# A fused attention, gated block and Fourier layer: the last 64 rows of a product by high and low parts side by side, and one tile of a norm loaded earlier

## The chip, the cores and the metric

The kernel runs on one core of one Trainium2 chip, in one launch. The metric is device microseconds of an execution; the median of three runs is given, and one more execution was recorded by the hardware profiler.

## The reference, cut to what matters

Three layers follow one another, all in fp32: attention in a window of 64, a gated block whose gate mixes over the sequence, and a Fourier layer with a norm and a feed-forward part. Batch is 4, the sequence S = 576, the model width 512.

```python
def _attn_ref(q, k, v):                     # (4, 8, 576, 64)
    ...                                     # softmax over rel in [0, 64)

def _moe_ref(x, w_in, w_spatial, b_spatial, w_out):
    h = np.maximum(x @ w_in, 0.0)           # w_in: 512 x 1024
    u, v = (h[..., :d_ff // 2], h[..., d_ff // 2:])
    v_n = (v - mean(v)) / np.sqrt(var(v) + 1e-06)
    v_s = np.einsum('ts,bsd->btd', w_spatial, v_n) + b_spatial[None, :, None]
    return (u * v_s) @ w_out

def _moe2_ref(x, w_ch1, w_ch2):             # w_ch1: 512 x 2048
    X = np.fft.fft(np.fft.fft(x, axis=1), axis=2)
    u = x + np.real(X)
    un = (u - mean(u)) / np.sqrt(var(u) + 1e-06)
    return u + np.maximum(un @ w_ch1, 0.0) @ w_ch2
```

## The kernel before, in words

**Precision.** Products are made of parts: a value is split into a rounded high part and the low rest, and a product of two values is three matmuls, high by high, high by low and low by high (`PASS`). `hi_lo` makes the parts: ACT copies the value into the high one, and one or two ticks later POOL (in places DVE) subtracts it from the value for the low one.

**One batch of the gated block.** x lies transposed in `xg`, 512 features on 4 x 128 partitions, with both parts. `b_v(b, m)` makes the value half for 128 rows (m = 0 to 3) or the last 64 (m = 4): 4 blocks of features by 3 passes, twelve matmuls of 512 columns into `ps_v` (L509). ACT takes the Relu into a `tr` buffer `vr` (L513), DVE the statistics of the norm (L487, L488), POOL the reciprocal root (L493, L494), DVE applies it in place (L498), and the parts go to the region `vn` of the resident array `ar`, those of the last 64 rows to its end, `vt` (L524 to L527). `b_u` makes the gate (`ps_u`, L539; ACT L542). `part_c` mixes over the sequence (`ps_c`, L552), then DVE multiplies by the gate into a `tr` buffer `gf` (L557), ACT copies its high part (L209) and POOL subtracts for the low one (L213). `part_d` is w_out (`ps_d`, L567). The Fourier steps follow.

**Buffers.** The pool `tr` has five buffers of 128 x 512 and one name for all of its users: `vr`, `gf`, the decoded weights `dec`, the norm's tiles `uu` and others. Weights come as 64-bit numbers: SP loads them (L222) into `raw_tile(0)`, `raw_tile(1)` or a staging buffer (all called `st`), ACT and DVE turn them into fp32 in a `dec` buffer (L230 to L243), and ACT and POOL make the parts (L209, L211). A raw tile holds two norm tiles of 128 x 512, its halves.

**The norm chains.** A tile of the Fourier layer's norm has four steps: `s0` loads 128 rows of `u_scr` (L754 on SP), `s1` takes the statistics on DVE and the root on POOL, `s2` applies them (DVE L498), `s3` transposes the tile on PE into `ps_un` (L783), and ACT and DVE make its parts (L787, L789). Chain 0 has three tiles, whose `s0` takes a `tr` buffer; chain 1 has three, in the halves of `raw_tile(1)` in turn.

**The order.** The engines' instructions stand in the order in which the program is written out. For each batch it follows a string, `ORDER_0` to `ORDER_3`: `i` is the next piece of the batch's block, `u` one of the gate, `s` a step of the next batch's attention, `n` one step of the weights' decoding, `a` a tick for what was put off, `c` and `d` the next step of chain 0 and of chain 1. Batch 3 has no attention beside it; there the weights of the feed-forward part are decoded and the chains' first tiles worked. The order of chain 0's steps comes from `staggered` (L884), that of chain 1 is a list (L898).

Of the kernel before, what the change touches and what calls it, by code (L numbers as in the profile page):

```python
# [9 lines left out]
F32 = mybir.dt.float32  # L10
# [3 lines left out]
AF = mybir.ActivationFunctionType  # L14
ALU = mybir.AluOpType
# [26 lines left out]
           "aannnnnnnaaaannannaaaiannaainninanniianaaaaaaaaaannsannnannnnnnnnnnananainnvnaasannnqv")  # L42
ORDER_1 = ("iiisuuuusiisuauquvqusiisiaiiiivsiiqvssaviiiasqaiasviaiiaiiiqsiiiiaiiiiiqsv")
ORDER_2 = ("iiisuuuusiisuauquvqusiisiaiiiivsiiqvssaviiiasaiasviaiqiaiiiqsiiiiaiiiiiqsv")
ORDER_3 = ("iniccnnncOiannuucnannnauucnnnnnnnnniciuucnnnunnaaaaaunanniddicaciciaaicaaaaaininindcindiniddaindinda"
           "idaindinidiiiiaidiaiiaiii")
ORDER = (ORDER_0, ORDER_1, ORDER_2, ORDER_3)

# [67 lines left out]
def tile_kernel(ctx: ExitStack, tc: tile.TileContext, q, k, v, w_in, w_sp, b_sp, w_out, w_c1, w_c2,  # L116
                rows, ident, mask, t1h, t1l, s2c, s2s, out):
    nc = tc.nc
    act, dve, pool, pe, sp = nc.scalar, nc.vector, nc.gpsimd, nc.tensor, nc.sync
# [5 lines left out]
    def raw_tile(i):  # L125
        return st_p.tile([128, 512], I64, tag=f"st{i}", name="st")
# [19 lines left out]
    def psO(nm="psO"):  # L146
        return ps_o.tile([128, 512], F32, tag="o", name=nm)

    def tr(nm, shape=(128, 512), dt=F32):
        return tr_p.tile(list(shape), dt, tag="tr", name=nm)  # L150
# [13 lines left out]
                 vn=5400, x0=4 * 2 * S, x1=4608)  # L164
    off, n = {}, 0
# [5 lines left out]
    def region(nm, o, n):  # L171
        return ar[:, off[nm] + o:off[nm] + o + n]

    wi = region("wi", 0, sizes["wi"]).rearrange("p (f k a c) -> p f k a c", f=8, k=4, a=2)
# [14 lines left out]
    PASS = ((0, 0), (0, 1), (1, 0))  # L189
# [4 lines left out]
    def later(n, fn):  # L194
        due.append((tick[0] + n, fn))
# [9 lines left out]
    def hi_lo(x, hi, lo, first=0, second=1, lo_eng=None):  # L205
        if first:
            later(first, lambda: act.activation(out=hi, in_=x, func=AF.Copy))
        else:
            act.activation(out=hi, in_=x, func=AF.Copy)  # L209
        if second == 0:  # L210
            (lo_eng or pool).tensor_tensor(out=lo, in0=x, in1=hi.bitcast(F32), op=ALU.subtract)  # L211
            return
        later(second, lambda: (lo_eng or pool).tensor_tensor(out=lo, in0=x, in1=hi.bitcast(F32), op=ALU.subtract))  # L213
# [270 lines left out]
    def norm_stats(x, n):  # L484
        st = sm_p.tile([128, 6], F32, tag="bn", name="bn")
        mv = sm_p.tile([128, 2], F32, tag="mv", name="mv")
        dve.bn_stats(out=st[0:n], in_=x[0:n])  # L487
        dve.bn_aggr(out=mv[0:n], in_=st[0:n])  # L488
        return mv

    def norm_rstd(mv, n):
        rs = sm_p.tile([128, 2], F32, tag="rs", name="rs")
        pool.tensor_scalar(out=rs[0:n, 0:1], in0=mv[0:n, 1:2], scalar1=1.0, scalar2=EPS, op0=ALU.mult, op1=ALU.add)  # L493
        pool.tensor_tensor(out=rs[0:n, 1:2], in0=rs[0:n, 0:1], in1=phalf[0:n], op=ALU.pow)  # L494
        return rs

    def norm_apply(x, mv, rs, n):
        dve.tensor_scalar(out=x[0:n], in0=x[0:n], scalar1=mv[0:n, 0:1], scalar2=rs[0:n, 1:2],  # L498
                          op0=ALU.subtract, op1=ALU.mult)

    def b_v(b, m):
        xt = xg[b % 2]
        n = 128 if m < 4 else 64
        ps = psO("ps_v")
        pf = ps.rearrange("p (f c) -> p f c", f=4)
        c = 0
        for kt in range(4):
            for a, w in PASS:
                pe.matmul(pf[0:n], lhsT=xt[:, kt, a, m * 128:m * 128 + n], rhs=wi[:, 4:8, kt, w],  # L509
                          start=(c == 0), stop=(c == 11))  # L510
                c += 1
        vr = tr("vr")
        act.activation(out=vr[0:n], in_=ps[0:n], func=AF.Relu)  # L513
        mv = norm_stats(vr, n)

        box = []
        later(1, lambda: box.append(norm_rstd(mv, n)))

        def finish():
            norm_apply(vr, mv, box[0], n)  # L520
            if m < 4:
                hi_lo(vr, vn[:, m, 0], vn[:, m, 1], 0, 1)
            else:
                act.activation(out=vt[0:64, 0], in_=vr[0:64], func=AF.Copy)  # L524
                act.activation(out=vt[0:64, 1], in_=vr[0:64], func=AF.Copy)
                pool.memset(vt[64:128, 1].bitcast(F32), 1.0)
                later(1, lambda: pool.tensor_tensor(out=vt[64:128, 0], in0=vr[0:64],  # L527
                                                    in1=vt[0:64, 0].bitcast(F32), op=ALU.subtract))

        later(2, finish)  # L530
# [183 lines left out]
    ff_slot, a2, un2, early_u, st2_ctx = {}, [], [], [], ExitStack()  # L714
# [4 lines left out]
    def un_parts(c):  # L719

        if c == 0:
            return [(0, 4, ar, at_x)]
        if c == 1:
            return [(0, 4, ar, at_y)]
        if c == 3:
            return [(0, 3, ar, at_x), (3, 4, ar, at_y + 1024)]
        return [(0, 2, un2[0], 0), (2, 3, ar, at_x + 3072), (3, 4, ar, at_y + 3072)]

    def un_of(c, part):
        m0, m1, x, o = part  # L730
        n = TILES[c] * 128
        return x[:, o:o + 2 * n * (m1 - m0)].rearrange("p (m a t) -> p m a t", a=2, t=n)
# [18 lines left out]
    def load_u(c, i, u=None):  # L751
        u = tr("uu") if u is None else u
        r0 = (FIRST[c] + i) * 128
        sp.dma_start(out=u, in_=u_scr[r0:r0 + 128, :])  # L754
        return u

    def norm_chain(c, i):
        box = {}

        def s0():  # L760
            if c == 1:
                if i == 0:
                    early_u.append(raw_tile(1).bitcast(F32))
                box["u"] = load_u(c, i, early_u[0][:, 512 * (i % 2):512 * (i % 2) + 512])
            else:
                box["u"] = load_u(c, i)

        def s1():
            box["mv"] = norm_stats(box["u"], 128)
            box["rs"] = norm_rstd(box["mv"], 128)  # L770

        def s2():
            norm_apply(box["u"], box["mv"], box["rs"], 128)

        def s3():
            u = box["u"]
            if c == 2 and not un2:
                st2_ctx.close()
                un2_p = ctx.enter_context(tc.tile_pool(name="un2", bufs=1))
                un2.append(un2_p.tile([128, 2048], F32R, name="un2"))  # L780
            ps = (psS if c == 2 else psT)("ps_un").rearrange("p (m c) -> p m c", m=4)
            for m in range(4):
                pe.transpose(ps[:, m, :], u[:, m * 128:(m + 1) * 128], idt)  # L783
            cc = slice(i * 128, i * 128 + 128)
            parts = [(un_of(c, p), ps[:, p[0]:p[1]]) for p in un_parts(c)]
            for un, x in parts:
                act.activation(out=un[:, :, 0, cc], in_=x, func=AF.Copy)  # L787
            for un, x in parts:
                dve.tensor_tensor(out=un[:, :, 1, cc], in0=x, in1=un[:, :, 0, cc].bitcast(F32), op=ALU.subtract)  # L789

        return [s0, s1, s2, s3]

    def ch1(c, j, h):
# [65 lines left out]
    with tc.manual_schedule():  # L859
# [19 lines left out]

        chain0, chain1 = ([norm_chain(c, i) for i in range(TILES[c])] for c in range(2))  # L880
        tables = (t1[:, 0], t1h), (t1[:, 1], t1l), (tc2, s2c), (ts2, s2s)
        chain_at = (0, 3, 4, 8)

        def staggered(chain):  # L884
            return [f[j] for n in range(40) for i, f in enumerate(chain) for j in range(4) if chain_at[j] + 6 * i == n]

        def start_w_out():
            st_next[:] = [lambda: raw_tile(0), lambda: raw_tile(1)]
            queue_units([w_out_unit(kt) for kt in range(4)])
            sp.dma_start(out=rix, in_=rows)  # L890
# [4 lines left out]
               "P": iter([lambda t=t: prep_w_sp(t) for t in range(5)]),  # L895
               "T": iter([lambda o=o, i=i: pool.dma_start(out=o, in_=i) for o, i in tables]),
               "b": iter([load_bias]), "B": iter([prep_bias]), "W": iter([start_w_out]),
               "O": iter([open_a2]), "c": iter(staggered(chain0)), "d": iter([chain1[i][j] for i, j in ((0, 0), (1, 0), (0, 1), (0, 2), (0, 3), (1, 1), (2, 0),  # L898
                                                            (1, 2), (1, 3), (2, 1), (2, 2), (2, 3))])}
        simple = {"s": attn_step, "n": nudge, "a": advance}  # L900
        for b in range(B):
# [12 lines left out]
        for g, group in enumerate(GROUPS):  # L914
# [7 lines left out]
            chain = [norm_chain(c, i) for c in nxt for i in range(TILES[c])]  # L922
            per = 2 if g == 0 else 3
            at = (0, 2, 3, 4) if g == 0 else (0, 1, 2, 3)
            start = N - 1 - at[3] - per * (len(chain) - 1)
            ul = {}
            for n in range(N + 1):
                if n < N:
                    c, j = steps[n]
# [51 lines left out]
```

## Time and profile before

| | |
|---|---|
| median of 3 runs | 815.94 us (815.81 to 817.22) |
| the profiled execution | 818.4 us, span 816.6 us |
| mean granted TensorE clock | 0.978 |
| PE busy | 783.4 us, 96% of the span |
| DVE, ACT, POOL busy | 414.8, 292.1, 238.8 us |

The rows below come from the profiled execution; their times count from the span's start. A row's bracket says how long the engine had stood idle before it and what ended that.

### The profile page before, as it was taken

What the parts mean: (1) busy time and instruction counts of PE and PEld (TensorE: products, weight loads), DVE (VectorE), ACT (ScalarE), POOL (GpSimd) and SP (SyncE); (2) the same over time, 40 slices, a digit from 0 to 9 for tenths busy, and PEclk for the clock granted to TensorE, in tenths of its full rate; (3) what the DMA queues carried; (4) which work ended last, traced back from release to release, by engine and by line L of the source; (5) the groups of instructions that cost most, each with busy time, mean ns of one, the idle gap of its engine ahead of it and who ended that gap; (6) DMA issues with size and microseconds to landing.
All of it is one profiled execution on the core that took longest, in us unless ns stands there. A gap on an engine that the chain in (4) does not pass through costs nothing.

```text
span 816.6 us, 13834 instructions
## 1 busy us (share of the span) xinstructions
PE 783.4 (96%) x5257; PEld 681.1 (83%) x5257; DVE 414.8 (51%) x1058; ACT 292.1 (36%) x867; POOL 238.8 (29%) x315
## 2 busy tenths in 40 slices
PE   6788999999999999997999999999999999999998
PEld 4557898889998999897889999888888888888886
DVE  3886765744473446565769888941212222221112
ACT  5556655545554544333433333320111111111100
POOL 1656462445424541444233333412000100010000
PEclk9679999999999999998999999999999999999999
DMA  8736426321223110422133445232000300020001
GB/s 207 178 71 173 125 62 166 92 49 43 58 71 73 31 27 26 137 91 65 50 134 116 125 126 154 77 117 78 14 14 13 116 14 13 14 78 26 0 1 51
DMA packets 89557, 62.79 MB, mean 77 GB/s; under 512 B 64978, under 2 KB 77522, under 8 KB 89492
## 3 DMA queue, kind: packets, MB, share of 16 engines
q1 hardware_dynamic: 87796, 55.29, 24.4%
q0 software_dynamic: 1696, 6.63, 2.4%
q8 instruction: 41, 0.67, 0.3%
q14 instruction: 24, 0.20, 0.1%
HBM read 52.47 MB, written 9.44 MB: 76 GB/s over the span
## 4 chain that ended last, share of the span: by engine, by line
PE 83%; DVE 7%; DMA 3%; ACT 3%; POOL 2%; issue 1%; SPq 1%; POOLq 0%; ACTq 0%; DVEq 0%
PE ps_y L824 24%; PE ps_h L800 24%; PE ps_v L509 6%; PE ps_d L567 5%; PE ps_c L552 4%; PE ps_u L539 4%; PE ps_x L446 3%; PE psS L396 2%; PE ps_pt L430 2%; PE ps_z L613 1%; PE ps_kn L371 1%; PE ps_z L621 1%; DVE dec L243 1%; PE ps_xt L639 1%; DMA kn<-in_k_dram 1%
## 5 line engine op out<-in xcount | busy, mean ns | idle before, releaser
L824 PE MATMUL ps_y<-ar 128*128 128x512 f32 x714 | 179.0, 391 | 0.0
L824 PEld LDWEIGHTS ps_y<-ar 128*128 128x128 f32 x714 | 133.4, 188 | 26.4
L800 PE MATMUL ps_h<-ar 128*128 128x384 f32 (+1 forms) x672 | 147.7, 365 | 0.1
L803 ACT ACTIVATE ar<-ps_h 128x512 fp32r<-128x512 f32 (+1 forms) x80 | 44.4, 555 | 281.2 <-PE ps_h L800 281.2
L804 DVE SCALAR_TENSOR_TENSOR ar<-ps_h,ar 128x512 fp32r<-128x512 f32 (+1 forms) x64 | 42.0, 656 | 193.0 <-ACT ar L803 193.0
L800 PEld LDWEIGHTS ps_h<-ar 128*128 128x128 f32 x672 | 122.0, 188 | 16.7 <-issue 0.7
L211 POOL TENSOR_TENSOR ar<-dec,ar 128x512 fp32r<-128x512 f32 x36 | 50.3, 1399 | 69.3 <-ACT ar L209 68.9
L509 PE MATMUL ps_v<-ar 128*128 128x512 f32 (+1 forms) x240 | 61.6, 411 | 2.6 <-POOL ar L211 1.1
L493 POOL TENSOR_SCALAR rs<-mv 128x1 f32<-128x1 f32 (+1 forms) x38 | 9.2, 243 | 185.2 <-DVE mv L488 184.9
L423 POOL TENSOR_TENSOR P<-P,r 128x384 f32<-128x384 f32 x48 | 39.8, 830 | 72.9 <-DVE r L422 37.2
L539 PE MATMUL ps_u<-ar 128*128 128x288 f32 x384 | 55.1, 300 | 2.7 <-ACT ar L450 2.7
L552 PE MATMUL ps_c<-ar 128*128 128x288 f32 x384 | 57.0, 298 | 0.5 <-DVE gf L557 0.5
L567 PE MATMUL ps_d<-ar 128*128 128x288 f32 x384 | 56.4, 305 | 1.0 <-POOL ar L211 1.0
L509 PEld LDWEIGHTS ps_v<-ar 128*128 128x128 f32 (+1 forms) x240 | 43.5, 185 | 16.5 <-POOL ar L211 1.7
L415 ACT ACTIVATE P<-P,nm 128x128 f32<-128x128 f32 x144 | 56.1, 398 | 2.9 <-DVE nm L406 2.9
L539 PEld LDWEIGHTS ps_u<-ar 128*128 128x128 f32 x384 | 52.0, 190 | 3.9 <-ACT ar L450 3.1
L567 PEld LDWEIGHTS ps_d<-ar 128*128 128x128 f32 x384 | 53.3, 196 | 1.4 <-POOL ar L211 1.4
L552 PEld LDWEIGHTS ps_c<-ar 128*128 128x128 f32 x384 | 52.3, 189 | 0.8 <-DVE gf L557 0.7
L406 DVE CUSTOM_DVE_ANT_0 P<-psS,msk 128x128 f32<-128x128 f32 x144 | 34.9, 279 | 33.7 <-PE psS L396 33.6
L800 PE MATMUL ps_h<-un,ar 128*128 128x512 f32 x168 | 44.0, 397 | 0.0
L800 PEld LDWEIGHTS ps_h<-un,ar 128*128 128x128 f32 x168 | 31.3, 188 | 7.1
L213 POOL TENSOR_TENSOR ar<-gf,ar 128x288 fp32r<-128x288 f32 x32 | 26.6, 835 | 32.5 <-ACT ar L209 32.5
(143 smaller groups left out, 1257.6 us busy)
## 6 DMA issues: line engine op xcount, KB each, us to landing
st<-in_moe_w_ch_dram SPq DMA_DIRECT2D x20, 512.0 KB, 3.6
uu<-u_scr SPq DMA_DIRECT2D x30, 256.0 KB, 2.6
uf<-in_moe_w_ch_dram SPq DMA_DIRECT2D x12, 512.0 KB, 3.8
va<-in_v_dram SPq DMA_DIRECT2D x40, 128.0 KB, 2.4
qn<-in_q_dram SPq DMA_DIRECT2D x48, 96.0 KB, 2.9
kn<-in_k_dram SPq DMA_DIRECT2D x36, 96.0 KB, 2.6
u_scr<-st SPq DMA_DIRECT2D x10, 256.0 KB, 2.0
uf<-in_moe_w_in_dram SPq DMA_DIRECT2D x4, 512.0 KB, 5.4
```

The source lines that it names most:

```text
L211: (lo_eng or pool).tensor_tensor(out=lo, in0=x, in1=hi.bitcast(F32), op=ALU.subtract)
L406: dve.tensor_tensor_reduce(out=P[:, r], in0=ps[:, r], in1=msk[:, int(g == 0 and r < 2)], scale=1.0, scalar=3.0e38, op0=ALU.add, op1=ALU.mi ...
L415: act.activation(out=P[:, r], in_=P[:, r], func=AF.Exp, scale=-1.0, bias=nm[:, r:r + 1], accum_out=sm[:, r:r + 1])
L423: lambda: pool.tensor_tensor(out=P, in0=P, in1=r.unsqueeze(2).to_broadcast([128, 3, 128]), op=ALU.mult))
L509: pe.matmul(pf[0:n], lhsT=xt[:, kt, a, m * 128:m * 128 + n], rhs=wi[:, 4:8, kt, w], start=(c == 0), stop=(c == 11))
L539: pe.matmul(ps[:, 0:HS], lhsT=wi[:, f, kt, w], rhs=xt[:, kt, a, t], start=(c == 0), stop=(c == 11))
L552: pe.matmul(ps[:, 0:HS], lhsT=vn[:, m, a, dd], rhs=ws[:, m, w, t], start=(c == 0), stop=False)
L567: pe.matmul(ps[:, 0:HS], lhsT=wo[:, kt, w, m * 128:(m + 1) * 128], rhs=G[:, kt, a, t], start=(c == 0), stop=(c == 11))
L800: pe.matmul(ps[:, 0:n_t], lhsT=w[:, 0, a, kt * 128:(kt + 1) * 128], rhs=un[kt][:, x, :], start=(n == 0), stop=(n == 11))
L803: act.activation(out=h[0], in_=ps[:, 0:n_t], func=AF.Relu)
L804: dve.scalar_tensor_tensor(out=h[1], in0=ps[:, 0:n_t], scalar=0.0, in1=h[0].bitcast(F32), op0=ALU.max, op1=ALU.subtract)
L824: pe.matmul(acc[i], lhsT=h[a][:, cc], rhs=w[:, 1, x], start=(j == 0 and z == 0), stop=(j == NFF - 1 and z == 2))
```

## The change

Two things. **First, the last 64 rows of the value half.** The high and the low part of x for these rows are copied side by side into `xtail` (a stretch of the region `vn`): 64 columns of high, 64 of low, for each block of features. One matmul then has 128 output rows, high above low, and eight matmuls (4 blocks by 2 parts of the weights) take the place of twelve; low by low comes along. Rows 64 to 127 of the result must be added to rows 0 to 63: ACT copies them to `vr`, DVE adds, and ACT takes the Relu in place. ACT makes the copy of the high parts, POOL that of the low ones, both written out in front of the fourth tile's Relu.

**Second, the norm's third tile.** Chain 0's third tile goes into half 1 of `raw_tile(1)` in place of a `tr` buffer, and its load is written out right behind those of the first two. Chain 1's second tile, which uses the same half, is loaded one weight load later, behind PE's transposes of that third tile. `ORDER_3` and the lists of steps follow.

```diff
-ORDER_3 = ("iniccnnncOiannuucnnannnauucnnnnnnnnniciuucnnnunnaaaaaunanniddicaciciaaicaaaaaininindcindiniddaindinda"
+ORDER_3 = ("iniccnnncOiannuuccnannnauucnnnnnnnnniciuucnnnunnaaaaaunannidiaciciaaicaaaaaininindcdindiniddaindinda"
...
+    xtail = region("vn", 4096, 512).rearrange("p (k a t) -> p k a t", k=4, a=2)
...
-        for kt in range(4):
-            for a, w in PASS:
-                pe.matmul(pf[0:n], lhsT=xt[:, kt, a, m * 128:m * 128 + n], rhs=wi[:, 4:8, kt, w],
-                          start=(c == 0), stop=(c == 11))
-                c += 1
         vr = tr("vr")
-        act.activation(out=vr[0:n], in_=ps[0:n], func=AF.Relu)
+        if m < 4:
+            for kt in range(4):
+                for a, w in PASS:
+                    pe.matmul(pf, lhsT=xt[:, kt, a, m * 128:m * 128 + n], rhs=wi[:, 4:8, kt, w],
+                              start=(c == 0), stop=(c == 11))
+                    c += 1
+            if m == 3:
+                act.activation(out=xtail[:, :, 0], in_=xt[:, :, 0, 512:576].bitcast(F32), func=AF.Copy)
+                pool.tensor_scalar(out=xtail[:, :, 1], in0=xt[:, :, 1, 512:576].bitcast(F32), scalar1=1.0, scalar2=0.0,
+                                   op0=ALU.mult, op1=ALU.add)
+            act.activation(out=vr, in_=ps, func=AF.Relu)
+        else:
+
+            for kt in range(4):
+                for w in range(2):
+                    pe.matmul(pf, lhsT=xtail[:, kt].rearrange("p a t -> p (a t)"), rhs=wi[:, 4:8, kt, w],
+                              start=(c == 0), stop=(c == 7))
+                    c += 1
+            act.activation(out=vr[0:n], in_=ps[64:128], func=AF.Copy)
+            dve.tensor_tensor(out=vr[0:n], in0=ps[0:n], in1=vr[0:n], op=ALU.add)
+            act.activation(out=vr[0:n], in_=vr[0:n], func=AF.Relu)
         mv = norm_stats(vr, n)
...
         def s0():
-            if c == 1:
-                if i == 0:
+            if (c, i) == (0, 2) or c == 1:
+                half = 1 if c == 0 else i % 2
+                if not early_u:
                     early_u.append(raw_tile(1).bitcast(F32))
-                box["u"] = load_u(c, i, early_u[0][:, 512 * (i % 2):512 * (i % 2) + 512])
+                box["u"] = load_u(c, i, early_u[0][:, 512 * half:512 * half + 512])
...
-               "O": iter([open_a2]), "c": iter(staggered(chain0)), "d": iter([chain1[i][j] for i, j in ((0, 0), (1, 0), (0, 1), (0, 2), (0, 3), (1, 1), (2, 0),
+               "O": iter([open_a2]), "c": iter([chain0[i][j] for i, j in ((0, 0), (0, 1), (0, 2), (1, 0), (2, 0), (0, 3), (1, 1), (1, 2),
+                                                            (1, 3), (2, 1), (2, 2), (2, 3))]), "d": iter([chain1[i][j] for i, j in ((0, 0), (0, 1), (1, 0), (0, 2), (0, 3), (1, 1), (2, 0),
```

The engines' orders at the places that matter. The line numbers of the kernel after are higher by 1 to 16.

ACT in batch 0, from the first decoding step ahead of the last 64 rows to `kT`, before:

```order
L230 ACTIVATE dec<-st 128x512
L542 ACTIVATE uf<-ps_u 128x288
L230 ACTIVATE dec<-st 128x512
L513 ACTIVATE vr<-ps_v 64x512
L288 ACTIVATE ar<-ps_ws 128x4x128
L290 ACTIVATE ar<-ps_ws_1154 64x128 x2
L372 ACTIVATE kT<-ps_kn 128x192
L377 ACTIVATE qT<-ps_qn 128x192
L415 ACTIVATE P,sm<-P,nm 128x128 x3
L542 ACTIVATE uf<-ps_u 128x288
```
And after:

```order
L231 ACTIVATE dec<-st 128x512
L558 ACTIVATE uf<-ps_u 128x288
L231 ACTIVATE dec<-st 128x512
L527 ACTIVATE vr<-ps_v 64x512
L529 ACTIVATE vr<-vr 64x512
L289 ACTIVATE ar<-ps_ws 128x4x128
L291 ACTIVATE ar<-ps_ws_1154 64x128 x2
L373 ACTIVATE kT<-ps_kn 128x192
L378 ACTIVATE qT<-ps_qn 128x192
L416 ACTIVATE P,sm<-P,nm 128x128 x3
L558 ACTIVATE uf<-ps_u 128x288
```
Behind the second decoding step one Relu stood (L513); a copy (L527) and a Relu (L529) stand there now, and between them DVE adds, so that the copies behind (L288, L289) and `kT` wait for DVE too.

DVE in batch 3, from the first product `gf` on, with the semaphores that each row waits for, before (`uu` is chain 0's third tile):

```order
L557 TENSOR_TENSOR gf<-ps_c,uf 128x288 [waits PE_49,Pool_49]
L789 TENSOR_TENSOR ar<-ps_un,ar 128x4x128 [waits Activation_49]
L557 TENSOR_TENSOR gf<-ps_c,uf 128x288 [waits PE_49,Pool_49]
L487 BN_STATS bn<-uu 128x6 [waits DMAHW1_49]
L488 BN_AGGR mv<-bn 128x2 [waits DVE_49]
L557 TENSOR_TENSOR gf<-ps_c,uf 128x288 [waits PE_49,Pool_49] x2
L498 TENSOR_SCALAR uu<-uu,mv,rs 128x512
L557 TENSOR_TENSOR gf<-ps_c,uf 128x288 [waits PE_49,Pool_49]
L243 SCALAR_TENSOR_TENSOR dec<-st,dec 128x512
L557 TENSOR_TENSOR gf<-ps_c,uf 128x288 [waits PE_49,Pool_49] x2
```
And after (the third tile is called `st` now):

```order
L573 TENSOR_TENSOR gf<-ps_c,uf 128x288 [waits PE_49,Pool_49]
L806 TENSOR_TENSOR ar<-ps_un,ar 128x4x128 [waits Activation_49]
L573 TENSOR_TENSOR gf<-ps_c,uf 128x288 [waits PE_49]
L488 BN_STATS bn<-st 128x6 [waits DMAHW2_49]
L489 BN_AGGR mv<-bn 128x2 [waits DVE_49]
L573 TENSOR_TENSOR gf<-ps_c,uf 128x288 [waits PE_49,Pool_49] x2
L499 TENSOR_SCALAR st<-st,mv,rs 128x512 [waits DMAHW6_49,DVE_49,Pool_49]
L573 TENSOR_TENSOR gf<-ps_c,uf 128x288 [waits PE_49,Pool_49]
L244 SCALAR_TENSOR_TENSOR dec<-st,dec 128x512
L573 TENSOR_TENSOR gf<-ps_c,uf 128x288 [waits PE_49,Pool_49] x2
```
The rows stand in the same order. The second `gf` waits for PE alone now, where it waited for POOL as well.

SP in batch 3, from the last store of `u_scr` on, where `L754` and `L770` load norm tiles and `L222` and `L223` weights, before:

```order
L673 DMA u_scr<-u 65x512
L754 DMA uu<-u_scr 128x512 x2
L222 DMA st<-in_moe_w_ch_dram 128x4x128
L222 DMA st<-in_moe_w_ch_dram 128x512
L222 DMA st<-in_moe_w_ch_dram 128x4x128
L222 DMA st<-in_moe_w_ch_dram 128x512
L222 DMA st<-in_moe_w_ch_dram 128x4x128
L754 DMA st<-u_scr 128x512 x2
L754 DMA uu<-u_scr 128x512
L222 DMA st<-in_moe_w_ch_dram 128x512
L222 DMA st<-in_moe_w_ch_dram 128x4x128
```
And after:

```order
L689 DMA u_scr<-u 65x512
L770 DMA uu<-u_scr 128x512 x2
L770 DMA st<-u_scr 128x512
L223 DMA st<-in_moe_w_ch_dram 128x4x128
L223 DMA st<-in_moe_w_ch_dram 128x512
L223 DMA st<-in_moe_w_ch_dram 128x4x128
L223 DMA st<-in_moe_w_ch_dram 128x512
L223 DMA st<-in_moe_w_ch_dram 128x4x128
L770 DMA st<-u_scr 128x512
L223 DMA st<-in_moe_w_ch_dram 128x512
L770 DMA st<-u_scr 128x512
```
The third tile's load moved from behind five weight loads and two tiles of chain 1 to right behind the first two; chain 1's second tile is behind one more weight load.

## Rows read from the trace of the kernel before

**Rows 1.** The page: busy time, share of the span and instructions of each engine.

```profile
PE 783.4 (96%) x5257; PEld 681.1 (83%) x5257; DVE 414.8 (51%) x1058; ACT 292.1 (36%) x867; POOL 238.8 (29%) x315
```
**Rows 2.** The timeline of PE in batch 3: start, time, line, operation, idle before.

```profile
367.87 1.87 PE L552 MATMUL ps_c<-ar 128*128 128x288 f32 x12 [0.48 <-DVE gf L557]
...
370.17 0.66 PE L783 MATMUL ps_un<-idt,uu 128*128 128x128 f32 x4 [0.17 <-DVE uu L498]
...
372.52 3.36 PE L567 MATMUL ps_d<-ar 128*128 128x288 f32 x24
379.73 1.09 PE L783 MATMUL ps_un<-idt,st 128*128 128x128 f32 x4 [3.85 <-DVE st L498]
```
**Rows 3.** Stretches: length; busy PE, PEld, DVE, ACT, POOL; granted clock; DMA share, GB/s.

```profile
53.00:62.00 9.00, 7.35 (x77) 5.38 (x77) 8.31 (x19) 5.93 (x22) 5.76 (x7) 1.00 0.14 31
...
74.95:78.20 3.25, 3.25 (x14) 3.05 (x15) 1.08 (x5) 1.49 (x6) 1.37 (x3) 0.50 1.02 337
...
379.73:387.54 7.81, 7.81 (x41) 7.81 (x41) 4.28 (x7) 2.11 (x6) 1.98 (x3) 0.63 0.33 103
387.54:392.67 5.13, 5.13 (x42) 5.05 (x40) 3.21 (x8) 2.25 (x8) 1.28 (x2) 1.00 0.00 0
```
**Rows 4.** The timeline of DVE in batch 3.

```profile
366.55 0.69 DVE L487 BATCH_NORM_STATS2 bn<-uu 128x6 f32<-128x512 f32 x1 [3.30 <-DMA uu<-u_scr]
...
367.38 0.44 DVE L557 TENSOR_TENSOR gf<-ps_c,uf 128x288 f32<-128x288 f32 x1
...
371.43 0.68 DVE L243 SCALAR_TENSOR_TENSOR dec<-st,dec 128x512 uint32<-128x512 uint32 x1
...
374.94 0.46 DVE L557 TENSOR_TENSOR gf<-ps_c,uf 128x288 f32<-128x288 f32 x1 [1.57 <-POOL ar L213]
...
378.47 1.11 DVE L498 TENSOR_SCALAR st<-st,mv,rs 128x512 f32<-128x512 f32 x1
```
**Rows 5.** The timelines of POOL and of SP's queue in batch 3.

```profile
372.84 1.30 POOL L211 TENSOR_TENSOR a<-dec,a 128x512 fp32r<-128x512 f32 x1
...
329.20 1.91 SPq L754 DMA_DIRECT2D uu<-u_scr  x2
...
360.89 0.37 SPq L754 DMA_DIRECT2D uu<-u_scr  x1
```
**Rows 6.** The timeline of PE in batch 0.

```profile
59.98 0.27 PE L446 MATMUL ps_x<-pt,va 128*64 128x64 f32 x1 [1.28 <-DVE pt L431]
...
74.95 1.68 PE L539 MATMUL ps_u<-ar 128*128 128x288 f32 x5 [2.40 <-ACT ar L450]
...
83.43 2.94 PE L509 MATMUL ps_v<-ar 128*64 128x512 f32 x12
86.21 0.60 PE L285 MATMUL ps_ws<-idt,w_sp 128*128 128x128 f32 x4
...
89.69 0.52 PE L430 MATMUL ps_pt<-idt,P 128*128 128x128 f32 x3 [0.35 <-ACT kT L372]
...
95.20 0.52 PE L430 MATMUL ps_pt<-idt,P 128*128 128x128 f32 x3 [0.72 <-DVE ar L295]
```
**Rows 7.** The timelines of ACT and then DVE in batch 0.

```profile
86.47 0.59 ACT L513 ACTIVATE vr<-ps_v 64x512 f32<-64x512 f32 x1 [0.36 <-PE ps_v L509]
...
89.22 0.33 ACT L372 ACTIVATE kT<-ps_kn 128x192 f32<-128x192 f32 x1 [1.23 <-PE ps_kn L371]
...
86.85 0.69 DVE L239 SCALAR_TENSOR_TENSOR dec<-st,dec 128x512 uint32<-128x512 uint32 x1
...
90.25 0.56 DVE L431 COPY pt<-ps_pt 128x384 f32<-128x384 f32 x1 [0.50 <-PE ps_pt L430]
```
**Rows 8.** The timelines of PE, DVE and ACT in batch 1.

```profile
182.12 6.60 PE L539 MATMUL ps_u<-ar 128*128 128x288 f32 x48
...
183.18 0.52 DVE L451 TENSOR_TENSOR ar<-ps_x,ar 128x384 fp32r<-128x384 f32 x1
...
179.03 0.60 ACT L513 ACTIVATE vr<-ps_v 128x512 f32<-128x512 f32 x1 [1.58 <-PE ps_v L509]
```

More of the change, by code (lines that the diff above doesn't have):

```diff
@@ L44 @@
 ORDER_2 = ("iiisuuuusiisuauquvqusiisiaiiiivsiiqvssaviiiasaiasviaiqiaiiiqsiiiiaiiiiiqsv")
-ORDER_3 = ("iniccnnncOiannuucnannnauucnnnnnnnnniciuucnnnunnaaaaaunanniddicaciciaaicaaaaaininindcindiniddaindinda"
+ORDER_3 = ("iniccnnncOiannuuccnannnauucnnnnnnnnniciuucnnnunnaaaaaunannidiaciciaaicaaaaaininindcdindiniddaindinda"
            "idaindinidiiiiaidiaiiaiii")
@@ L881, in tile_kernel @@
         tables = (t1[:, 0], t1h), (t1[:, 1], t1l), (tc2, s2c), (ts2, s2s)
-        chain_at = (0, 3, 4, 8)
-        def staggered(chain):
-            return [f[j] for n in range(40) for i, f in enumerate(chain) for j in range(4) if chain_at[j] + 6 * i == n]
         def start_w_out():
```

## The prediction

> **What bounds the kernel now.** I read the page first, for which engine fills the span: PE is busy 783.4 us of 816.6 [rows 1], so a change pays in two ways only, by fewer matmuls or by shorter waits of PE. Then I looked for waits of PE near the two places that the change touches. In batch 3, where the spatial mix and w_out run beside the first normalisation tiles, PE waits 0.48 us for the third `gf`, 0.17 for a normalised tile and then 3.85 for the normalised first tile of chain 1, at 379.73 [rows 2]. The table by stretches shows what that last wait costs besides: the granted clock is 0.63 of full in the stretch behind it (a mean between its levels of 1.2 and 2.4 GHz), and four transposes with 36 matmuls take 7.81 us, against 5.13 for the same work after the second tile [rows 3]. So the wait costs 3.85 + 2.68 us. DVE's timeline tells what made DVE late: its statistics at 366.55 stood 3.30 us for the DMA that brings the third tile of chain 0 [rows 4], and that DMA was issued only at 360.89, behind weight loads [rows 5]. Behind it the `gf` products go one by one with POOL.
>
> At the value half's tail I read PE, ACT and DVE in batch 0 [rows 6, 7] and batch 1 [rows 8], for the slack that its results have now. In batch 0 PE waits at 89.69 for ACT's `kT` and at 95.20 for DVE; nothing is spare there.
>
> **Matmuls.** Twelve matmuls of 512 columns run from 83.43 to 86.21 [rows 6], 0.232 us each. Four fewer per batch give 0.93 us. They are now 128 wide in the stationary side; the columns that pass stay 512, so I keep 0.232.
>
> The Trainium skill, page "TensorE: Matmul & The Clock Gate", section "Back-to-back issue gap", gives about 131 ns for 512 columns in a sustained stream. By that four matmuls would be worth an estimated 0.52 us and the batches 2.1 in place of 3.7; the trace disagrees, with 0.232 us in each such run, and decides.
>
> **The new steps.** ACT's copy out of PSUM replaces a Relu of the same shape: 0.59 [rows 7]. The second Relu, SBUF to SBUF, is not in the trace in this form; between `kT`'s 0.33 for 192 columns and 0.59 for 512 [rows 7] I take 0.59, the same number of columns. DVE's add lies between 0.52 for 384 columns from PSUM [rows 8] and 0.69 for a three-operand pass of 512 [rows 7]: 0.66. So the tail's statistics come some 1.9 us after its last matmul plus waits, 1.3 later than now counted from there. The two copies into `xtail` need only x, which is there before; ACT's (256 columns, 0.33 to 0.59) fits into its 1.58 us of idle before the fourth Relu [rows 8]. POOL's I bound by 0 and its 1.30 for a 512-column pass [rows 5]; the fourth tile's twelve matmuls cover either, and I take nothing. Without that cover the last product would start up to 1.3 late.
>
> **Batch 0.** ACT is free at 86.11 (86.47 less its idle 0.36), so the copy runs to 86.6. DVE is in decoding until 87.46, so the add waits behind it and runs to 88.1, the Relu to 88.7, and the statistics start 1.33 later than at 87.46. ACT's next copies stand behind the Relu: ACT, free at 87.99 (89.22 less 1.23), is free at about 89.7, so `kT` is some 0.4 later and PE, which gets there 0.93 sooner, waits 1.6 in place of 0.35. On DVE the idle 0.50 before the `pt` copy [rows 7] takes up part of the 1.33; 0.83 goes on to the normalised tail. ACT's next copy of it has about 0.14 to spare; 0.69 passes to the last DVE step for which PE waits at 95.20. So batch 0 ends 0.69 later, not 0.93 earlier. Bounds: -0.93 if all is covered, +1.33 if nothing is.
>
> **Batches 1 and 2.** DVE is free when the tail ends. The next thing on it, the low half of `ps_x`, ran 183.18 to 183.70 and comes about 0.44 later, 184.14 with its latency. PE needs it for the third group of gate matmuls: 182.12 plus half of 6.60 [rows 8], less 0.93, is 184.48. The cover holds by 0.3: -0.93 each. Batch 2's row has the same shape. Without the cover each would lose up to the same 0.69.
>
> **Batch 3.** PE gains 0.93 at the tail; the extra add and the later statistics push DVE by about 0.45 there, as in batch 1. DVE's second `gf` ended at 363.25 (366.55 less 3.30); now 363.7. The third tile's load now stands right behind the two at 329.20 on SP, some 30 us before 360.89 [rows 5], so the statistics follow at once and the third `gf` comes at about 364.5 in place of 367.38 [rows 4]. PE's 0.48 and 0.17 vanish. PE then arrives at 372.52 + 3.36 - 0.93 - 0.48 - 0.17 = 374.30.
>
> DVE's side: with the buffer that the third tile gave up, a `gf` waits for POOL's low half of the one before last, no longer of the last. The fifth stands behind the normalise, which runs 366.0 to 367.1 with the 1.11 that it took beside POOL at 378.47; the decode's sign step (0.68) ends at 368.1 [rows 4], ACT's high copy of that weight at 368.7, POOL's 1.30 for its low half [rows 5] at 370.1. The seventh `gf` waits for that: 370.1 in place of 374.94. From there to the transpose the order is unchanged, 379.73 - 374.94 = 4.79, so the transpose comes at 374.9. PE waits 0.6 in place of 3.85. A wait of 1.28 us at 59.98 [rows 6] left the clock at 1.00 in the stretch around it [rows 3], so the work behind goes at 5.13, not 7.81. Sum of batch 3: -0.93 - 0.48 - 0.17 - 3.25 - 2.68 = **-7.5**.
>
> What is late next: the load of chain 1's second tile now stands on SP behind a weight load which waits for that sign step, and for PE's transposes of the third tile. It goes out at about 369. Even at the 5.7 us that the load at 360.89 took to reach the statistics at 366.55 it is there at 374.9, before DVE asks at about 376.4. No cost; cover 1.5 us. The early load itself delays five weight loads by one tile's load; the two behind which SP still waits for a free staging buffer set their own time, so I count nothing.
>
> **Sum.** +0.69 - 0.93 - 0.93 - 7.51 = -8.7. The profiled execution took 818.4 us (span 816.6), 2.5 above the median of the three runs; it would go to 809.7, and the median of 815.94 to **807.3**. Feed-forward behind is PE's own stream and shifts along.
>
> **Rivals.**
> - *The `gf` chain stays serial.* The freed buffer goes to decoded weights, which share the pool, and each `gf` goes on waiting for POOL's last low half. At 1.89 us a step (374.94 less 367.38, by four) the seventh comes at about 372.0 and the transpose at 376.8: a wait of 2.5. After a wait of 2.40 at 74.95 [rows 6] the clock was 0.50 [rows 3], so the 2.68 isn't saved. Batch 3 gives -2.9, the sum -4.1: **811.8**. For it: that the pool is shared, and that the seventh stood 1.57 for POOL [rows 4]. Against it: the order shows the second without that wait. Chance 0.2.
> - *Batch 0's wait drops the clock.* 1.6 lies between the 1.28, which did not, and the 2.40, which did. The stretch behind 74.95 ran 3.25 us at 0.50, some 1.6 lost: **808.9**. Chance 0.15.
> - *Slower.* The chain copy, add, Relu ends on PE's path in all four batches as in batch 0, 0.69 each, and the early load moves nothing since POOL's work, not the DMA, set the 379.73. That is +2.8: **818.7**. It decides if DVE is more than 0.3 later in batches 1 and 2 than I counted. Against it: the 3.30 us of idle ended by that DMA. Chance 0.04.
> - *It does not do what it says*: another load keeps the third tile's place as the last thing awaited, and batch 0's loss eats what the matmuls give. About **815**. Chance 0.05.
>
> **How the numbers follow.** Forecast 0.56, rivals 0.2, 0.15, 0.04, 0.05. The least time, with batch 0 covered (-1.62) and no wait at the transpose (-0.6), is 805.1; the range 805.0 to 812.0 takes in the first two rivals too. A measurement can tell about 0.2% (1.6 us) from no change: faster 0.91, same 0.05, slower 0.04.
>
> **What would show it.** PE's wait at chain 1's first transposes under 1 us and the clock at 1.00 behind it; no DMA wait on DVE between the second and third `gf`; eight matmuls in the tail, near 1.86 us; PE's wait for `kT` in batch 0 grown to about 1.6. I am wrong if that transpose still waits over 2 us, if PE waits for DVE at the third gate group of batches 1 and 2, or if chain 1's second tile arrives after 376.

## The result and the profile after

The kernel after took 808.93 us (808.76 to 810.21, four runs) against 816.12 (815.81 to 817.22) for the kernel before on the same chip: a ratio of 0.9913, with an interval of 0.9896 to 0.993. The gain is 7.2 us; the forecast was 8.7, to 807.3 us, which lies just outside what the interval allows (5.7 to 8.5). PE's busy time went from 783.4 us [rows 1] to this line of the page of the kernel after (its span is 808.4):

```profile
PE 776.6 (96%) x5241; PEld 677.6 (84%) x5241; DVE 419.5 (52%) x1062; ACT 295.9 (37%) x875; POOL 241.7 (30%) x319
```
To see where the time went I compare the two profiled executions: at the ends of four stages I subtract PE's start times for the same group of matmuls, after less before. From then on to the last feed-forward product PE's distance stays at -8.8 us; nothing is lost or gained in the second half. What lies before 80.74 is left out, since up to there the programs are the same but for the two copies into `xtail`, and so is the stretch from 95.20 to 133.50, in which a wait for the load of q and k differs by 0.4 (in the runs below this stretch differs by -1.0 to +0.3).

| stage, by the time in the kernel before | forecast | after |
|---|---|---|
| batch 0's tail, 80.74 to 95.20 | +0.69 | +0.63 |
| batch 1, 133.50 to 210.64 | -0.93 | -0.96 |
| batch 2, 210.64 to 297.17 | -0.93 | -0.91 |
| batch 3, 297.17 to 387.54 | -7.51 | -6.35 |
| sum | -8.68 | -7.59 |

One thing must be known to read the times of single runs: the thirteen traces of this case reach the place of 80.74 between 76.77 and 81.39 us, and two of the kernel after at 79.96 and 77.30, though up to there the programs are nearly the same. Much of that can be TensorE's clock in the first attention steps. These rows are from the profile of before and from a second one of the kernel after (run 9); PE does nearly the same part of the program in both, in 3.8 us less in the second (columns as in [rows 3]: length, five busy times, granted clock):

```profile
36.00:52.00 16.00, 13.33 (x113) 10.05 (x114) 12.54 (x36) 7.64 (x28) 7.75 (x9) 0.57 0.50 123
```
```profile
36.00:48.00 12.00, 8.30 (x102) 6.17 (x101) 11.45 (x31) 6.82 (x24) 6.66 (x8) 1.00 0.64 153
```
So whole times decide to within a microsecond or two here, and the stages of the traces the rest.

**Batch 0.** PE's timeline after, where [rows 6] stand before:

```profile
82.64 2.02 PE L524 MATMUL ps_v<-ar 128*128 128x512 f32 x8
84.49 0.60 PE L286 MATMUL ps_ws<-idt,w_sp 128*128 128x128 f32 x4
...
89.47 0.55 PE L431 MATMUL ps_pt<-idt,P 128*128 128x128 f32 x3 [1.84 <-ACT kT L373]
...
95.05 0.52 PE L431 MATMUL ps_pt<-idt,P 128*128 128x128 f32 x3 [0.80 <-DVE ar L296]
```
Eight matmuls take 82.64 to 84.49, 0.231 us each. PE then waits 1.84 us for `kT` where it waited 0.35, and 0.80 in place of 0.72 for DVE: the 0.93 that PE won and 0.63 more. ACT's timeline and then DVE's show the chain behind it: the add on DVE, ACT's Relu that waited 1.41 us for it, the statistics that waited for the Relu, and `kT` behind the Relu on ACT:

```profile
87.38 0.63 ACT L529 ACTIVATE vr<-vr 64x512 f32<-64x512 f32 x1 [1.41 <-DVE vr L528]
...
89.09 0.33 ACT L373 ACTIVATE kT<-ps_kn 128x192 f32<-128x192 f32 x1
...
86.67 0.68 DVE L528 TENSOR_TENSOR vr<-ps_v,vr 64x512 f32<-64x512 f32 x1
88.04 0.69 DVE L488 BATCH_NORM_STATS2 bn<-vr 64x6 f32<-64x512 f32 x1 [0.70 <-ACT vr L529]
```

**Batch 3.** PE's timeline after, where [rows 2] stand before:

```profile
366.22 0.60 PE L800 MATMUL ps_un<-idt,st 128*128 128x128 f32 x4
...
368.52 3.32 PE L583 MATMUL ps_d<-ar 128*128 128x288 f32 x24
373.52 0.63 PE L800 MATMUL ps_un<-idt,st 128*128 128x128 f32 x4 [1.69 <-DVE st L499]
...
378.74 0.60 PE L800 MATMUL ps_un<-idt,st 128*128 128x128 f32 x4
```
The two small waits for `gf` and the third tile are gone, and the 3.85 at chain 1's first transposes became 1.69. The 36 matmuls behind it now go at the full clock. The table by stretches of the kernel after says so for both long waits; the first line is the stretch behind batch 0's 1.84, the second, where 0.63 stood in [rows 3], that behind the 1.69:

```profile
89.47:92.10 2.63, 2.63 (x21) 2.41 (x21) 2.63 (x13) 1.79 (x9) 2.46 (x4) 1.00 0.31 70
...
373.50:378.70 5.20, 5.17 (x40) 5.20 (x41) 4.23 (x7) 2.10 (x6) 2.02 (x3) 1.00 0.43 134
```
DVE's timeline shows the third tile's statistics at once behind the second `gf`, with no wait for a DMA, where 3.30 us of idle stood in [rows 4]:

```profile
361.31 0.68 DVE L488 BATCH_NORM_STATS2 bn<-st 128x6 f32<-128x512 f32 x1
...
362.13 0.44 DVE L573 TENSOR_TENSOR gf<-ps_c,uf 128x288 f32<-128x288 f32 x1
...
367.89 0.46 DVE L573 TENSOR_TENSOR gf<-ps_c,uf 128x288 f32<-128x288 f32 x1 [1.58 <-POOL a L212]
368.26 0.65 DVE L235 TENSOR_SCALAR dec<-dec 128x512 f32<-128x512 f32 x1
368.94 1.05 DVE L236 TENSOR_SCALAR dec<-dec 128x512 uint32<-128x512 uint32 x1
369.91 0.68 DVE L488 BATCH_NORM_STATS2 bn<-st 128x6 f32<-128x512 f32 x1
```
and POOL's, the two low halves that run beside DVE's two decoding steps (L235, L236; each of these ends 0.28 us behind the low half beside it):

```profile
367.81 0.82 POOL L214 TENSOR_TENSOR ar<-gf,ar 128x288 fp32r<-128x288 f32 x1
368.90 0.81 POOL L214 TENSOR_TENSOR ar<-gf,ar 128x288 fp32r<-128x288 f32 x1 [0.27 <-ACT ar L210]
```

### The profile page after: what moved, and what is told of

Same layout as the page of the kernel before. It is cut to its first block, busy times and chain, and to the rows that moved or that the text cites. A ratio compares the mean times of both kernels' runs of the same rounds, so it can differ in the third digit from the quotient of the medians.

```text
span 808.4 us, 13814 instructions
## 1 busy us (share of the span) xinstructions
PE 776.6 (96%) x5241; PEld 677.6 (84%) x5241; DVE 419.5 (52%) x1062; ACT 295.9 (37%) x875; POOL 241.7 (30%) x319
## 4 chain that ended last, share of the span: by engine, by line
PE 83%; DVE 7%; ACT 3%; DMA 2%; POOL 2%; issue 1%; SPq 1%; POOLq 0%; ACTq 0%; DVEq 0%
PE ps_y L841 24%; PE ps_h L817 24%; PE ps_c L568 5%; PE ps_v L512 5%; PE ps_d L583 5%; PE ps_u L555 4%; PE ps_x L447 2%; PE psS L397 2%; PE ps_pt L431 2%; DMA qn<-in_q_dram 2%; PE ps_z L629 1%; PE ps_kn L372 1%; PE ps_z L637 1%; PE ps_c L571 1%; PE ps_xt L655 1%
## 5 line engine op out<-in xcount | busy, mean ns | idle before, releaser
L583 PE MATMUL ps_d<-ar 128*128 128x288 f32 x384 | 54.1, 297 | 1.0 <-POOL ar L212 1.0
L512 PE MATMUL ps_v<-ar 128*128 128x512 f32 x192 | 50.3, 416 | 2.6 <-POOL ar L212 1.2
L583 PEld LDWEIGHTS ps_d<-ar 128*128 128x128 f32 x384 | 51.0, 188 | 1.4 <-POOL ar L212 1.4
L512 PEld LDWEIGHTS ps_v<-ar 128*128 128x128 f32 x192 | 37.0, 198 | 12.2 <-POOL ar L212 1.7
```

Of the source, the lines that this page charges most:

```text
L512: pe.matmul(pf, lhsT=xt[:, kt, a, m * 128:m * 128 + n], rhs=wi[:, 4:8, kt, w], start=(c == 0), stop=(c == 11))
L583: pe.matmul(ps[:, 0:HS], lhsT=wo[:, kt, w, m * 128:(m + 1) * 128], rhs=G[:, kt, a, t], start=(c == 0), stop=(c == 11))
```

## The experiments

The stages of all runs, worked out as above, in us against the kernel before; batch 3 in its two parts, up to chain 1's first transposes (379.73) and from there to the second (387.54):

| run | batch 0 | 1 | 2 | 3, to the first | to the second | sum |
|---|---|---|---|---|---|---|
| kernel after | +0.63 | -0.96 | -0.91 | -3.76 | -2.59 | -7.6 |
| 1 tail alone | +0.62 | -0.92 | -0.96 | +0.63 | -1.04 | -1.7 |
| 2 norm alone | -0.03 | -0.01 | -0.01 | -4.30 | -2.59 | -6.9 |
| 3 load late | +2.07 | -0.97 | -0.96 | -2.76 | -1.16 | -3.8 |
| 4 buffer held | +0.62 | -0.96 | -0.96 | -3.25 | -1.06 | -5.6 |
| 5 tail in 1 and 2 | 0.00 | -0.92 | -0.96 | -4.33 | -2.59 | -8.8 |
| 6 decoding behind | +2.08 | -0.90 | -0.98 | -5.61 | -1.13 | -6.5 |
| 7 Relu on DVE | +0.42 | -0.99 | -0.95 | -3.97 | -2.59 | -8.1 |
| 8 runs 5 and 6 | 0.00 | -0.89 | -0.97 | -5.24 | -2.17 | -9.3 |

**1. The tail alone.** The kernel before, with only the hunk of `b_v` and `xtail`:

```diff
+    xtail = region("vn", 4096, 512).rearrange("p (k a t) -> p k a t", k=4, a=2)
...
+                    pe.matmul(pf, lhsT=xtail[:, kt].rearrange("p a t -> p (a t)"), rhs=wi[:, 4:8, kt, w],
+                              start=(c == 0), stop=(c == 7))
```

> The kernel before with the side-by-side tail alone; the norm's third tile is loaded as before. My theory: batch 0 +0.6, batches 1 and 2 -0.93 each, and batch 3 nothing, since the wait at 379.73 belongs to DVE's chain behind the late load, so that PE's 0.93 is waited away and DVE's extra work (0.45 to 0.6) may even come on top: 814.9 to 815.5 us. Rival (the parts add, the tail's 0.93 counts in batch 3 too): 814.0.

Measured: 815.97 us, ratio 1.0006 (0.9987 to 1.0025): no gain, half a microsecond above the expected range, and the rival's 814.0 lies just outside the interval. PE's row at chain 1's first transposes:

```profile
377.27 0.80 PE L799 MATMUL ps_un<-idt,st 128*128 128x128 f32 x4 [3.83 <-DVE st L499]
```
The wait is as long as before, and with batch 3's tail PE's 0.93 is gone: the transposes come 0.63 later. DVE's added work stands on that path, PE's matmuls don't. The stages are those of my theory. The stretch behind was 1.04 us shorter at the same wait; its granted clock was 0.75 in the table by stretches, against 0.63 [rows 3], so I don't count that as the tail's.

**2. The norm alone.** The kernel after with the twelve matmuls and one Relu put back everywhere:

```diff
-        if m < 4:
...
+        for kt in range(4):
+            for a, w in PASS:
+                pe.matmul(pf[0:n], lhsT=xt[:, kt, a, m * 128:m * 128 + n], rhs=wi[:, 4:8, kt, w],
+                          start=(c == 0), stop=(c == 11))
+                c += 1
```

> The kernel after with the tail's twelve matmuls and single Relu put back in all batches; the third tile stays early. My theory: with both parts PE waits 1.69 us for chain 1's first tile because DVE is 0.6 later by the tail's add and PE 0.93 earlier; without the tail that wait is about 0.2 and batch 3 gains 6.9 us, so 809.2 us, hardly above the kernel after. Rival (parts add, the norm is worth the 5.4 that are left when 0.93 is taken off batch 3's 6.35): 810.7.

Measured: 810.49 us against 815.68, ratio 0.9925 (0.9907 to 0.9944). By the whole time that is the rival's figure. The stage says otherwise: batch 3 gains 6.89, against 6.35 with the tail, and PE waits 0.70 at the transposes, where 0.2 were expected:

```profile
375.02 0.63 PE L784 MATMUL ps_un<-idt,st 128*128 128x128 f32 x4 [0.70 <-DVE st L498]
```
I take the stage, since batches 0 to 2 are here as before, within 0.03, and the whole times spread more than the 1.5 us between theory and rival: the tail costs 0.54 in batch 3. Run 5 tests it a second time.

**3. The load late again, the buffer still free.** The step that loads the third tile stands behind the weight loads, into the raw half as in the kernel after:

```diff
-ORDER_3 = ("iniccnnncOiannuuccnannnauucnnnnnnnnniciuucnnnunnaaaaaunannidiaciciaaicaaaaaininindcdindiniddaindinda"
+ORDER_3 = ("iniccnnncOiannuucnannnauucnnnnnnnnniciuucnnnunnaaaaaunannidicaciciaaicaaaaaininindcdindiniddaindinda"
...
-"c": iter([chain0[i][j] for i, j in ((0, 0), (0, 1), (0, 2), (1, 0), (2, 0), (0, 3), (1, 1), (1, 2),
+"c": iter([chain0[i][j] for i, j in ((0, 0), (0, 1), (0, 2), (1, 0), (0, 3), (1, 1), (1, 2), (2, 0),
```

> The kernel after, but the third tile's load stands behind the five weight loads again, directly behind chain 1's first tile, still into the raw half, so that the freed buffer stays. If the load's place is what matters: DVE waits 2 to 3 us for the DMA between the second and the third gf, PE's wait for chain 1's first tile grows from 1.69 to 3.5 or more and the clock falls behind it: 812.5 to 814. If the freed buffer is what matters: 810 or less.

Measured: 813.22 us, ratio 0.9959 (0.9936 to 0.9982). Batch 3 gains 3.92 in place of 6.35. DVE's row of the statistics, then PE's of chain 1's first transposes:

```profile
364.36 0.69 DVE L488 BATCH_NORM_STATS2 bn<-st 128x6 f32<-128x512 f32 x1 [1.43 <-DMA st<-u_scr]
...
376.10 1.09 PE L800 MATMUL ps_un<-idt,st 128*128 128x128 f32 x4 [2.71 <-DVE st L499]
```
The DMA is awaited 1.43 us, less than expected (the load stands behind one tile of chain 1 here, behind two in the kernel before), and PE's wait is 2.71, not 3.5. That the whole time lies in the expected range may have another reason in part: in the profiled execution batch 0's stage lost 1.44 more than in the kernel after (run 6 shows why). Behind PE's wait the clock is lower, in the table by stretches:

```profile
376.00:382.70 6.70, 6.61 (x40) 6.64 (x41) 4.38 (x7) 2.13 (x7) 2.08 (x3) 0.76 0.39 120
```
**4. The load early, the buffer held.** The normalise writes to a buffer of the pool taken at the statistics:

```diff
+            if (c, i) == (0, 2):
+                box["o"] = tr("uu")
             box["mv"] = norm_stats(box["u"], 128)
...
+                dve.tensor_scalar(out=box["o"], in0=box["u"], scalar1=box["mv"][:, 0:1], scalar2=box["rs"][:, 1:2],
+                                  op0=ALU.subtract, op1=ALU.mult)
+                box["u"] = box["o"]
```

> The kernel after, but the third tile's normalised values are written to a buffer of the shared pool, taken at the statistics, so that the gf products have one buffer less, as before, while the load stays early. If the buffer matters: the gf products stand 1.85 us apart, the seventh comes 1.7 later and the wait for chain 1's first tile goes from 1.69 to about 3.4: 810.6, or 813.2 if the clock falls behind it. If only the load matters: 808.9.

Measured: 811.98 us, ratio 0.9951 (0.9933 to 0.9969). Batch 3 gains 4.31. DVE from the seventh `gf` on, POOL's low half beside the second decoding step, then PE's transposes:

```profile
366.54 0.46 DVE L573 TENSOR_TENSOR gf<-ps_c,uf 128x288 f32<-128x288 f32 x1 [1.56 <-POOL ar L214]
366.91 0.42 DVE L235 TENSOR_SCALAR dec<-dec 128x512 f32<-128x512 f32 x1
367.37 0.43 DVE L236 TENSOR_SCALAR dec<-dec 128x512 uint32<-128x512 uint32 x1
...
367.56 0.90 POOL L214 TENSOR_TENSOR ar<-gf,ar 128x288 fp32r<-128x288 f32 x1 [1.05 <-ACT ar L210]
...
371.33 0.63 PE L807 MATMUL ps_un<-idt,st 128*128 128x128 f32 x4 [2.22 <-DVE st L499]
```
From the second `gf` (358.22 here, 360.94 after) to the seventh it takes 8.32 us, against 6.95 in the kernel after: the buffer is worth 1.37 there. But the two decoding steps take 0.42 and 0.43, not 0.65 and 1.05, which gives 0.85 of it back, so the wait is only 2.22. POOL's low half comes here 0.19 behind the start of the second step and leaves it at 0.43; in the kernel after it comes 0.04 ahead of it. This run is nearly the first rival of the prediction, built: a wait of 2.5 was forecast for it, and a gain of 2.9 in batch 3. The clock fell partly all the same: the stretch behind is 1.5 us longer than in the kernel after. So load and buffer both count: without the one batch 3 gives back 2.4 us of its 6.35, without the other 2.0, and 1.4 and 1.5 of that is the slower stretch behind the wait.

**5. The tail where DVE is free.** The new tail in batches 1 and 2 alone:

```diff
-        if m < 4:
+        if m < 4 or b in (0, 3):
...
-            if m == 3:
+            if m == 3 and b not in (0, 3):
```

> The kernel after with the side-by-side tail in batches 1 and 2 alone; batches 0 and 3 have the twelve matmuls and the single Relu. My theory (the tail pays where DVE is free and costs where DVE ends PE's next wait): batch 0 is 0.63 us shorter than in the kernel after, batch 3 0.55, so 807.7 us. Rival (each product less is 0.93 of PE wherever it stands): 1.86 more than the kernel after, 810.8.

Measured: 807.34 us, ratio 0.9901 (0.9884 to 0.9918). Batch 0 is as before, and batch 3 gains 6.92, as in run 2. PE's wait at chain 1's first transposes is 0.67, as without any tail (0.70 in run 2). These are the theory's figures, and the rival's 810.8 is out.

**6. The decoding behind the normalise.** Two `n` in the order string are moved, in the kernel after:

```diff
-ininindcdindiniddaindinda
+ininidcdidnniniddaindinda
```

> The kernel after with two decoding steps of DVE (clamp and shift of one weight, 1.70 us beside POOL, and the merge of the low word, 0.68) moved from in front of chain 1's first normalise to behind it. My theory (the 1.69 us wait that is left at chain 1's first transposes is DVE's, and half of it the decoding that runs beside POOL's bunched low halves): that wait falls under 0.3; the second tile's wait may grow to at most 0.5; 807.2 to 808.0 us. Rival (POOL's low halves and the gf chain set it): the wait stays above 1.4, 808.9.

Measured: 810.33 us (808.0 to 812.25), ratio 0.993 (0.9909 to 0.995), where 807.2 to 808.0 was expected. The wait at chain 1's first transposes is gone; one of 1.33 us stands at the second tile's:

```profile
374.05 0.60 PE L800 MATMUL ps_un<-idt,st 128*128 128x128 f32 x4
374.40 4.99 PE L583 MATMUL ps_d<-ar 128*128 128x288 f32 x36
380.73 0.63 PE L800 MATMUL ps_un<-idt,st 128*128 128x128 f32 x4 [1.33 <-DVE st L499]
```
DVE caused the first wait, as I had it. But the steps that were moved ran beside POOL in their new place, and held up the second tile by more than the 0.5 that I had allowed; batch 3 gains 6.74, 0.39 more than the kernel after. The whole time is higher all the same. In the profiled execution (812.25) that comes in part from batch 0, whose code is that of the kernel after: behind the same wait for `kT` (1.85) this execution ran at the low clock, and the stage lost 2.08 in place of 0.63:

```profile
89.78:93.30 3.52, 3.52 (x16) 3.52 (x17) 3.44 (x13) 1.30 (x7) 2.77 (x5) 0.53 0.34 64
```
That is the second rival of the prediction, seen in this execution and in that of run 3 (2.07), and not in those of runs 1 and 4 or of the kernel after.

**7. The Relu on DVE.**

```diff
-            act.activation(out=vr[0:n], in_=vr[0:n], func=AF.Relu)
+            dve.tensor_scalar(out=vr[0:n], in0=vr[0:n], scalar1=0.0, scalar2=0.0, op0=ALU.max, op1=ALU.add)
```

> The kernel after with the tail's Relu on DVE, right behind its add, in place of ACT. My theory (in batch 0 DVE sets the end, ACT's kT only the first of two waits): PE's wait for kT falls from 1.84 to about 0.3, that for DVE at the next transposes grows from 0.80 to about 2.1, the end moves by 0.2; with batch 3's DVE 0.2 earlier 808.5 us. Rival (the round trip over ACT is the cost): batch 0 gains 1.5, 807.4.

Measured: 808.85 us, ratio 0.9917 (0.9901 to 0.9934). PE in batch 0:

```profile
88.13 0.55 PE L431 MATMUL ps_pt<-idt,P 128*128 128x128 f32 x3 [0.26 <-ACT kT L373]
...
95.08 0.52 PE L431 MATMUL ps_pt<-idt,P 128*128 128x128 f32 x3 [1.70 <-DVE ar L296]
```
The wait for `kT` fell to 0.26, that for DVE grew to 1.70, and the stage lost 0.42 where it had lost 0.63. The 0.2 was as expected; the wait for DVE had been put at 2.1. DVE sets the end of this stage, as the theory had it, and ACT's long wait in front was not the price.

**8. Both.** Runs 5 and 6 in one:

> Both: the side-by-side tail in batches 1 and 2 alone, and the two decoding steps behind chain 1's first normalise. My theory: PE has no wait left at chain 1's first transposes, the 0.70 of the norm part alone goes too: 807.0 us, below both kernels. Rival (the decoding held back is paid later, at the feed-forward's first weights or at the second tile): 807.7 or more.

Measured: 807.61 us (806.14 to 810.71), ratio 0.9911 (0.9892 to 0.993). Batch 3 gains 7.41, the most of all. PE has no wait at the first transposes and 0.31 at the second:

```profile
369.04 0.60 PE L800 MATMUL ps_un<-idt,st 128*128 128x128 f32 x4
369.39 4.99 PE L583 MATMUL ps_d<-ar 128*128 128x288 f32 x36
374.68 0.63 PE L800 MATMUL ps_un<-idt,st 128*128 128x128 f32 x4 [0.31 <-DVE st L499]
```
The theory's 807.0 and the rival's 807.7 lie closer together than single executions do, so the whole time decides nothing. By the stages the wait at the first transposes is gone, as the theory had it, and part of it comes back as the 0.31 at the second tile, as the rival had it; the sum is 0.5 better than run 5's.

**9 to 11. The candidates beside the kernel after, on one chip.** Three kernels that had run before, unchanged.

> The kernel after unchanged, beside the two versions that should beat it, on one chip. By the stages of the profiles it is 1.2 us above the version with the tail in batches 1 and 2 alone: 808.9 us.

> The version with the tail in batches 1 and 2 alone, beside the kernel after on one chip: 807.5 us if what its profile's stages show holds (0.63 less in batch 0, 0.57 less in batch 3); the same as the kernel after if the profiles' single executions misled.

> That version with the two decoding steps behind chain 1's first normalise, beside the kernel after: 0.5 us below the version without, 807.0 us, by the stages of its profile; 807.5 if the decoding held back is paid in other executions.

Measured, each against 815.93 us for the kernel before: the kernel after 807.55 us (0.9906, 0.9879 to 0.9933), the tail in batches 1 and 2 alone 808.33 (0.9903, 0.9873 to 0.9933), both edits 807.59 (0.99, 0.9875 to 0.9926). The stages repeat: +0.64, -0.91, -0.98, -6.39 for the kernel after; -0.03, -0.90, -0.97, -6.92; and -0.02, -0.89, -0.95, -7.28. By their sums the two versions are 1.2 and 1.5 us better. The whole times, expected at 808.9, 807.5 and 807.0, don't show it: executions differ by more than that before 80.74. Whether they beat the kernel after in time stays open.

An early load of the third tile into a buffer of the pool was not tried; that such a buffer, held from there on, would leave the other users of the pool waiting for one another is argued, not shown.

## Why the prediction was right, and where a size was off

- **Matmuls**: 0.231 us each, forecast 0.232; -0.96 and -0.91 in batches 1 and 2. The price was the row's; the 131 ns of the Trainium skill's page "TensorE: Matmul & The Clock Gate", section "Back-to-back issue gap", isn't seen here.
- **Batch 0**: +0.63 for +0.69. The wait for `kT` was 1.84, not 1.6 (the forecast's own terms, 0.35 + 0.93 + 0.4, make 1.7; its copy that "runs to 86.6" ends at 86.7 by its own figures, and nothing hung on that). Its chain, copy, add, Relu behind DVE's decoding, is what the trace shows, and run 7 shows that DVE, not ACT, ends the stage. The rival that this wait drops the clock was not this execution's, but runs 3 and 6 had it, behind 1.84 and 1.85 us: at that length the clock is open. The median of 808.93 is that rival's 808.9 by chance only, as far as the trace tells: there the clock stayed, and what is missing from the forecast is in batch 3.
- **Batch 3, the mechanism**: the DMA wait between the second and third `gf` vanished, PE's 0.48 and 0.17 too, and the clock stayed at 1.00 behind the shortened wait. Runs 3 and 4 show that load and buffer both count. Two signs of being wrong did not come: PE has no wait inside the gate matmuls of batches 1 and 2, and DVE none for chain 1's second tile.
- **Batch 3, the size**: the term that was off is PE's wait at chain 1's first transposes, 1.69 in place of 0.6. The step that failed was "From there to the transpose the order is unchanged, 379.73 - 374.94 = 4.79": the order is, the durations aren't. In the kernel after it took 373.52 - 367.89 = 5.63 us, since DVE's L235 and L236 took 0.65 and 1.05. In the kernel before and in runs 1 and 4, where the `gf` products stand apart, they took 0.42 and 0.43; in all seven traces that have the second buffer and the old order of the steps, 0.64 to 0.65 and 1.05 to 1.06. With a second buffer POOL's low halves come bunched, one beside each step, and the second (0.81, at 368.90) begins just ahead of L236. That is 0.84 of the 1.1; the rest is the seventh `gf`, which comes 0.26 later, counted from PE's arrival, than replayed.
- What I had not weighed: the tail's 0.93 in batch 3 was counted as won and isn't (run 1 and run 5). Behind the shortened wait DVE is the bound, and there the tail costs 0.54 (run 2 against the kernel after). The forecast sum hid that, because it let PE wait only 0.6.

The Trainium skill, page "SBUF — State Buffer", section "Who interferes with whom", says that DVE and GpSimd share a port pair under an exclusive lock. The trace agrees in direction: L236 is 0.62 us longer beside a pass of 0.81.

## What to carry to other kernels

A matmul saved is worth its time only where the engine that works up its result is not what PE waits for next: the same edit gave 0.9 us in each of two batches and cost about 0.6 in each of the two others. A replay that moves work closer together must price it beside its new neighbours; a row's duration holds for the neighbours that it had. And where a wait of PE is long enough to slow the clock behind it, the last half microsecond taken off can pay several times over: from 2.22 us of wait in run 4 to 1.69 batch 3 gained 2.0.

## What the runs showed of the hardware

- Behind a wait of PE the granted clock is not a function of the wait's length alone in these traces: 1.84 us left it at 1.00 in the kernel after and gave 0.53 in run 3 (89.17 to 92.65 there), in the same code. The stretch behind chain 1's first transposes, 5.2 us at the full clock, took 1.5 us more behind 2.22 (run 4), 1.4 behind 2.71 (run 3), 1.6 behind 3.83 (run 1) and 2.6 behind 3.85 (the kernel before).
- DVE's two decoding steps on SBUF took 0.42 and 0.43 us with POOL idle (the first two rows, of the kernel after) and 1.03 and 1.40 beside POOL's passes in run 6. There POOL's pass had begun first each time, and each step ended 0.3 us behind it, as the timelines of DVE and then of POOL show. In run 4, where DVE's step had begun first, it kept its 0.43, and POOL's pass took 0.90 in place of 0.80 to 0.82:

```profile
357.37 0.42 DVE L235 TENSOR_SCALAR dec<-dec 128x512 f32<-128x512 f32 x1
357.82 0.43 DVE L236 TENSOR_SCALAR dec<-dec 128x512 uint32<-128x512 uint32 x1
```
```profile
373.47 1.03 DVE L235 TENSOR_SCALAR dec<-dec 128x512 f32<-128x512 f32 x1
374.54 1.40 DVE L236 TENSOR_SCALAR dec<-dec 128x512 uint32<-128x512 uint32 x1
```
```profile
373.30 0.93 POOL L214 TENSOR_TENSOR ar<-gf,ar 128x288 fp32r<-128x288 f32 x1 [0.33 <-ACT ar L210]
374.18 1.47 POOL L212 TENSOR_TENSOR a<-dec,a 128x512 fp32r<-128x512 f32 x1
```
